# Start-up order, constants, and a last block in two column halves in a fused attention and mixture-of-experts kernel

## The chip, the cores and the metric

The kernel runs on one core of one Trainium2 chip. The metric is device microseconds of one execution; three runs of the kernel before are given, with their median. The profile is of one further execution, with a time of its own.

The engines are named as the profile names them: PE multiplies matrices (PEld is its weight load), DVE, ACT and POOL work on rows, SP issues plain transfers. Indirect transfers (gathers and scatters of rows) are issued by POOL.

## The reference

```python
scores = (q_c @ k_c.T) / sqrt(64)                 # chunks of 64 positions, per head
attn = exp(scores - scores.max(-1)); attn /= attn.sum(-1)
x = (attn @ v_c)                                  # 4608 tokens of 512
out = x.copy()
do_compute = (x @ w_skip) > 0
xc = x[do_compute]
e_idx = argmax(xc @ w_gate); gate_w = softmax(xc @ w_gate)[e_idx]      # 8 experts
for e in range(8):
    h = relu(xc[e_idx == e] @ w1[e])              # 512 -> 1024
    out[those rows] = xc[...] + gate_w * (h @ w2[e])                   # 1024 -> 512
```

## The kernel before

Attention runs over 36 tiles of 128 tokens, with heads side by side. An outer loop over i, from -1 to 40, writes one step of each stage per turn, for different tiles: scores of tile i+1 (`pe_scores`, L226, in float32, 32 small matmuls), their row maximum (`ve_max`, DVE), its subtraction by two matmuls into the same bank (`pe_sub`, L242), the exponential (`ac_exp`, ACT), the transpose of tile i-1 (`pe_ptrans`) and its eviction (`ac_pt`, ACT), the product with v (`pe_pv`), the division (`ve_norm`, DVE), the transpose of the result (`pe_xtrans`), its split into two float16 parts (`ac_xt`, ACT and POOL) and the routing logits of tile i-4 (`pe_logits`, L311). The product with v and the logits share a tile `pv` of which there is one; `pe_logits` of one tile opens it for the product of the next, so it waits until `ve_norm` has read the product before. Each engine takes its instructions in the order in which this loop writes them.

The first loads stand ahead of the loop (L163 to L173); those of later tiles are written inside it, up to three tiles ahead, each bound to the last PE instruction written so far (`paced`). Ten matmuls on zeros (`pe_warm`, L192) run on PE before the first scores. A table of constants `csb` is loaded in turn 1 (L721) and converted by `more_constants` (L209) in turn 3; the logits need its `wgs`.

From the logits groups of tiles are routed to the experts; each expert's tokens are gathered in blocks of at most 128 rows (`fetch`), transposed (`blk_xt`), multiplied with w1 (`l1_steps`) and w2 (`l2_steps`), added to the rows (`blk_out`) and scattered. Weights are split into two float16 parts, so each product is three matmuls. Blocks 0 to 3 of the first expert are computed between attention steps by a generator (`filler`); a block is open once so many half turns have passed since its gather was written: `cur[0] >= fetched[m] + F_LAG[min(m, EARLY_B)]`, with `F_LAG = (7, 6, 6, 5)` and `EARLY_B = 3`. Block 3 has 80 rows; its banks are named `eb`, those of the blocks before `fb`.

The other experts follow the attention loop, expert by expert. The last one has a single block of 112 rows. After it come a loop over blocks that overflow (`tc.For_i`, L938), whose body has no row in this trace, and behind the loop the output of the last block:

```python
    while len(prev) > 1:
        out_prev()
    ...
    with tc.For_i(0, lend, 1) as si:
        ...
    out_prev(1 << 30)
```

`prev` holds the generators of `blk_out` that are not finished; before, only that of the last block is left when the loop comes.

Of the kernel before, what the change touches and what calls it, by code (L numbers as in the profile page):

```python
# [18 lines left out]
P = 128  # L19
# [4 lines left out]
DM = H * D  # L24
# [35 lines left out]
NPRE = 18  # L60
F_LAG = (7, 6, 6, 5)
F_RATE = 1.05
# [45 lines left out]
def moe_attention_kernel(ctx: ExitStack, tc: tile.TileContext, q: bass.AP, k: bass.AP, v: bass.AP, cst: bass.AP, wall: bass.AP, out: bass.AP):  # L108
# [43 lines left out]

    def load_k(t, eng=None):
        if t < NT:
            paced((eng or nc.sync).dma_start(T[t]["qk"][:, 1], k[t]))

# [6 lines left out]
    load_q(0)  # L163
    load_k(0, nc.scalar)
    load_q(1)
    load_k(1)
    load_v(0)
    load_q(2)
    load_k(2)
    load_v(1)  # L170
    load_q(3)
    load_k(3)
# [18 lines left out]

    pe_warm(10)  # L192

# [11 lines left out]
    wgs = cpool.tile([P, KC, 2, NX], F16, name="wgs")  # L205
    reci = cpool.tile([P, NB], I32, name="reci")
    recg = cpool.tile([P, NB], F32, name="recg")

    def more_constants():  # L209
        nc.vector.tensor_copy(upper, C("upper"))  # L210
        nc.vector.tensor_copy(iota, C("iota"))
        nc.vector.tensor_scalar(wgs[:, :, 0], wg, SR, None, op0=ALU.mult)
        nc.vector.scalar_tensor_tensor(wgs[:, :, 1], wg, SR, wgs[:, :, 0], op0=ALU.mult, op1=ALU.subtract)
        nc.gpsimd.tensor_copy(vals[:, :, 0], C("tok"))
        nc.gpsimd.tensor_copy(vals[:, :, 2], C("part").to_broadcast([P, NT]))
        nc.gpsimd.memset(ecum[:, 0, :], 0.0)
        nc.gpsimd.memset(rec, 0.0)
# [220 lines left out]
    def finish_records(lo, hi):  # L438
        nc.vector.scalar_tensor_tensor(reci[:, lo:hi], rec[:, 0, lo:hi], EMPTY, rec[:, 2, lo:hi], op0=ALU.add, op1=ALU.add)
        nc.vector.tensor_tensor(recg[:, lo:hi], rec[:, 1, lo:hi], rec[:, 3, lo:hi], op=ALU.add)  # L440
        nc.vector.tensor_scalar(recg[:, lo:hi], recg[:, lo:hi], 1.0 / (SGATE * SX * SW * SW), None, op0=ALU.mult)
        ready.append(hi)

# [93 lines left out]

    def l2_steps(y, ht, w, o, n, every=2):
        cg = l2_tiles(n)
        fw = FC // cg  # L540
        for f in range(fw):
            for m, (a, b) in enumerate(((0, 0), (0, 1), (1, 0))):
                for c in range(cg):
                    fc = c * fw + f
                    pe_last[0] = nc.tensor.matmul(y[c * P // cg:c * P // cg + n], ht[:, a, fc, o:o + n], w[:, b, fc, P * KC:], start=(f == 0 and m == 0), stop=(f == fw - 1 and m == 2), skip_group_check=True)  # L545
            if (f + 1) % every == 0:
                yield

    def blk_out(ys, parts, idx, gate, xg, n, rows=NTOK):
        yo = spool.tile([P, DM], F32, name="yo", bufs=3)  # L550
        for (o, m), y in zip(parts, ys):
            cg = l2_tiles(m)
            r = slice(o, o + m)
            for c in range(cg):
                nc.vector.scalar_tensor_tensor(yo[r], y[c * P // cg:c * P // cg + m], gate[r], yo[r] if c else xg[r], op0=ALU.mult, op1=ALU.add)  # L555
                yield
        rows_dma(out=out[:rows, :], out_offset=bass.IndirectOffsetOnAxis(ap=idx[:n], axis=0), in_=yo[:n], in_offset=None, bounds_check=rows - 1, oob_is_err=False)

# [135 lines left out]
    for i in range(-1, NT + 5):  # L694
# [22 lines left out]
        if i == 0 or i > 1:  # L717
            load_k(i + LOOK + (i == 0))
        on(pe_scores, i + 1)
        if i == 1:  # L720
# [4 lines left out]
        run_route("d", 600 if urgent() else 350 if not late_group() else 0)  # L725
        on(ve_max, i + 1)
        flush()
        on(pe_logits, i - 4, i - 1 if i - 1 < NT else None)
# [11 lines left out]
        fill(F_RATE if i < NT else 2)  # L740
        if i == 3:
            more_constants()
        move(extra[1:2])
        for u in CONV.get(i, ""):
# [142 lines left out]
    for u, (p, bs, offs, n) in list(enumerate(units))[1:]:  # L887
# [20 lines left out]
        for b_, o in zip(bs, offs):  # L908
            ys = []
            for po, m in parts[b_]:  # L910
                y = ps_y.tile([P, DM], F32, name="y")
# [90 lines left out]
```

## Time and profile before

| | |
|---|---|
| median of 3 runs | 338.68 us (335.71 to 340.44) |
| the profiled execution | 336.04 us, span 334.3 us |
| granted PE clock, mean | 0.994 |
| PE busy | 314.5 us, 94% of the span |
| DVE, ACT, POOL busy | 237.0, 162.6, 152.3 us |
| moved by DMA | 81.83 MB, 245 GB/s over the span |

Times of an engine are the union of its instructions. PE's instructions overlap, and their ends are modelled; a PE that is busy is not PE at its peak. What an engine waited for is inferred from semaphores.

### The profile page before, as it was taken

What the parts mean: (1) busy time and instruction counts of PE and PEld (TensorE: products, weight loads), DVE (VectorE), ACT (ScalarE), POOL (GpSimd) and SP (SyncE); (2) the same over time, 40 slices, a digit from 0 to 9 for tenths busy, and PEclk for the clock granted to TensorE, in tenths of its full rate; (3) what the DMA queues carried; (4) which work ended last, traced back from release to release, by engine and by line L of the source; (5) the groups of instructions that cost most, each with busy time, mean ns of one, the idle gap of its engine ahead of it and who ended that gap; (6) DMA issues with size and microseconds to landing.
All of it is one profiled execution on the core that took longest, in us unless ns stands there. A gap on an engine that the chain in (4) does not pass through costs nothing. (4 is left out here: it accounts for less than half of the span.)

```text
span 334.3 us, 11290 instructions
## 1 busy us (share of the span) xinstructions
PE 314.5 (94%) x4537; PEld 221.7 (66%) x4537; DVE 237.0 (71%) x566; ACT 162.6 (49%) x337; POOL 152.3 (46%) x187
## 2 busy tenths in 40 slices
PE   7989899989999998989999999999999999999991
PEld 3777777877777776656555447647647649688580
DVE  1667676685679788853489876886887999868330
ACT  2555344655565462434467454554554555456120
POOL 5166478879987971188920441231242221120111
PEclk9999999999999999999999999999999999999997
DMA  7989799999999999587823897667567676744010
GB/s 263 336 274 319 252 283 298 378 329 284 308 393 324 381 393 370 221 261 267 255 63 125 263 305 231 208 201 232 188 225 253 199 225 224 246 167 154 34 30 28
DMA packets 41320, 81.83 MB, mean 245 GB/s; under 512 B 5022, under 2 KB 5022, under 8 KB 41264
## 3 DMA queue, kind: packets, MB, share of 16 engines
q1 hardware_dynamic: 38016, 71.48, 63.7%
q0 software_dynamic: 3104, 9.33, 8.5%
q8 instruction: 37, 0.61, 0.7%
q10 hardware_dynamic: 144, 0.26, 0.2%
q14 instruction: 19, 0.16, 0.1%
HBM read 67.02 MB, written 14.17 MB: 243 GB/s over the span
## 5 line engine op out<-in xcount | busy, mean ns | idle before, releaser
L545 PE MATMUL y<-wset,ht 128*128 128x512 f16 (+7 forms) x480 | 86.2, 380 | 0.0
L486 POOL DMA_INDIRECT out<-yo,reci x22 | 24.3, 1104 | 129.9 <-DVE yo L555 115.7
L520 PEld LDWEIGHTS <-wset 128*128 128x128 f16 x768 | 64.1, 98 | 15.5 <-issue 2.6
L545 PEld LDWEIGHTS <-ht 128*128 128x128 f16 (+7 forms) x552 | 44.8, 101 | 42.3 <-issue 2.0
L796 DVE SCALAR_TENSOR_TENSOR wset<-wst,wset 128x512 f16<-128x512 f32 x96 | 61.5, 683 | 0.9 <-ACT wset L795 0.4
L520 PE MATMUL hp<-xt,wset 128*128 128x288 f16 (+4 forms) x576 | 60.5, 267 | 0.0
L795 ACT ACTIVATE wset<-wst 128x512 f16<-128x512 f32 x96 | 53.9, 620 | 3.3 <-DVE wset L796 2.2
L524 ACT ACTIVATE ht<-hp 128x288 f16<-128x288 f32 (+5 forms) x56 | 21.7, 389 | 44.5 <-PE hp L520 43.3
L239 DVE TENSOR_REDUCE mx<-sp 128x8 bf16<-128x512 f32 x36 | 24.7, 686 | 23.0 <-PE sp L234 22.9
L249 ACT ACTIVATE px<-sp 128x512 f32<-128x512 f32 x36 | 21.4, 594 | 33.6 <-PE sp L245 28.2
L512 DVE SCALAR_TENSOR_TENSOR ht<-hp,ht 128x288 f16<-128x288 f32 (+5 forms) x56 | 23.5, 428 | 17.3 <-ACT ht L524 15.4
L309 POOL TENSOR_TENSOR xh<-xs,xh 128x256 f16<-128x256 f32 (+1 forms) x45 | 34.3, 779 | 2.2
L261 ACT ACTIVATE pts<-pt 128x512 f32<-128x512 f32 x36 | 21.4, 596 | 28.1 <-PE pt L256 28.1
L273 PE MATMUL pv<-vb,pts 64*64 64x65 f32 x1152 | 27.3, 224 | 2.5 <-issue 2.2
L306 POOL CAST xh<-xs 128x512 f16<-128x512 f32 x27 | 17.0, 629 | 24.2 <-ACT xs L305 24.0
L234 PEld LDWEIGHTS sp<-qkb 64*64 64x64 f32 x1152 | 20.6, 135 | 10.9 <-ACT px L249 5.2
L234 PE MATMUL sp<-qkb 64*64 64x64 f32 x1152 | 25.7, 225 | 1.1 <-issue 0.7
L486 POOL DMA_INDIRECT xg<-out,reci x22 | 23.9, 1089 | 5.8 <-issue 4.4
L273 PEld LDWEIGHTS pv<-vb,pts 64*64 64x64 f32 x1152 | 21.5, 133 | 4.4 <-issue 3.5
L500 ACT ACTIVATE xt<-xq 128x512 f16<-128x512 f32 (+6 forms) x18 | 9.1, 512 | 29.4 <-PE xq L499 28.9
L256 PE MATMUL pt<-ident,px 128*128 128x128 f32 x144 | 22.6, 279 | 0.1
L555 DVE SCALAR_TENSOR_TENSOR yo<-y,recg,xg 128x512 f32<-128x512 f32 (+7 forms) x20 | 14.8, 742 | 7.6 <-PEq L938 5.0
(133 smaller groups left out, 461.3 us busy)
## 6 DMA issues: line engine op xcount, KB each, us to landing
wst<-in_wall SPq DMA_DIRECT2D x96, 256.0 KB
vb<-in_v SPq DMA_DIRECT2D x36, 260.0 KB
qkb<-in_q SPq DMA_DIRECT2D x36, 256.0 KB
qkb<-in_k SPq DMA_DIRECT2D x35, 256.0 KB
out<-hold SPq DMA_DIRECT2D x20, 256.0 KB
wset<-in_wall SPq DMA_DIRECT2D x16, 256.0 KB
out<-xb SPq DMA_DIRECT2D x16, 256.0 KB
wset<-in_wall SPq DMA_DIRECT2D x8, 512.0 KB
```

Of the source, the lines that this page charges most:

```text
L234: pe_last[0] = nc.tensor.matmul(sp[halves[a], c, j * CH:(j + 1) * CH], qk[halves[c], 0, w], qk[halves[c], 1, w], start=(j == 0), stop=Fals ...
L239: nc.vector.tensor_reduce(mx, T[t]["sp"][:, :, :KC * CH].rearrange("p c (j s) -> p c j s", s=CH), axis=AX.X, op=ALU.max, negate=True)
L256: pe_last[0] = nc.tensor.transpose(pt[:, j, :], px[:, j * P:(j + 1) * P], ident)
L273: pe_last[0] = nc.tensor.matmul(pv[halves[c], jj, m * VW:(m + 1) * VW], pt[halves[jj], c * 2 + jp, halves[a]], vv[halves[jj], c * KC + m, ...
L309: nc.gpsimd.tensor_tensor(xh[:, 1, w], xs[:, w], xh[:, 0, w], op=ALU.subtract)
L486: ins = nc.gpsimd.indirect_dma_start(**kw)
L512: nc.vector.scalar_tensor_tensor(ht[:, 1, fc, :n], hp, 0.0, ht[:, 0, fc, :n], op0=ALU.max, op1=ALU.subtract)
L520: pe_last[0] = nc.tensor.matmul(hp, w()[:, a, fc, j * P:(j + 1) * P], xt[:, b, j, :n], start=(m == 0), stop=(m == 11))
L524: nc.scalar.activation(ht[:, 0, fc, :n], hp, AF.Relu)
L545: pe_last[0] = nc.tensor.matmul(y[c * P // cg:c * P // cg + n], ht[:, a, fc, o:o + n], w[:, b, fc, P * KC:], start=(f == 0 and m == 0), st ...
L795: nc.scalar.activation(w[:, 0, fc, r], st[part], AF.Copy, scale=SW)
L796: nc.vector.scalar_tensor_tensor(w[:, 1, fc, r], st[part], SW, w[:, 0, fc, r], op0=ALU.mult, op1=ALU.subtract)
```

## The change

Six edits. (1) The first loads all go through SP, in the order q0, k0, q1, k1, q2, k2, v0, q3, v1, k3, v2. (2) Nine matmuls on zeros in place of ten. (3) The scores of tile 1 are written in turn -1, behind those of tile 0, ahead of the first subtraction. (4) `wgs` is made in turn 2 by ACT and POOL (not in turn 3 by DVE); the rest of the constants in turn 5 by ACT and POOL. (5) `F_LAG` of block 3 is 6 half turns, not 5. (6) The last block's second layer runs as two halves of 256 columns, each with its own bank, output and scatter; the row numbers of the scatter are doubled (`recl`) and the output is seen as rows of 256.

```diff
-F_LAG = (7, 6, 6, 5)
+F_LAG = (7, 6, 6, 6)
...
     load_q(0)
-    load_k(0, nc.scalar)
+    load_k(0)
     load_q(1)
     load_k(1)
-    load_v(0)
     load_q(2)
     load_k(2)
+    load_v(0)
+    load_q(3)
     load_v(1)
-    load_q(3)
     load_k(3)
     load_v(2)
...
-    pe_warm(10)
+    pe_warm(9)
...
+    recl = cpool.tile([P, 2], I32, name="recl")
...
     def more_constants():
-        nc.vector.tensor_copy(upper, C("upper"))
-        nc.vector.tensor_copy(iota, C("iota"))
-        nc.vector.tensor_scalar(wgs[:, :, 0], wg, SR, None, op0=ALU.mult)
-        nc.vector.scalar_tensor_tensor(wgs[:, :, 1], wg, SR, wgs[:, :, 0], op0=ALU.mult, op1=ALU.subtract)
+        nc.scalar.activation(wgs[:, :, 0], wg, AF.Copy, scale=SR)
+        nc.gpsimd.tensor_scalar(wg, wg, SR, 1.0, op0=ALU.mult, op1=ALU.mult)
+        nc.gpsimd.tensor_tensor(wgs[:, :, 1], wg, wgs[:, :, 0], op=ALU.subtract)
+
+    def row_constants():
+        nc.scalar.activation(upper, C("upper"), AF.Copy)
+        nc.scalar.activation(iota, C("iota"), AF.Copy)
         nc.gpsimd.tensor_copy(vals[:, :, 0], C("tok"))
...
+        if hi == NB:
+            for z in range(2):
+                nc.vector.tensor_scalar(recl[:, z:z + 1], reci[:, NB - 1:], 2.0, float(z), op0=ALU.mult, op1=ALU.add)
...
-    def l2_steps(y, ht, w, o, n, every=2):
+    def l2_steps(y, ht, w, o, n, every=2, cols=(0, DM)):
...
-                    pe_last[0] = nc.tensor.matmul(y[c * P // cg:c * P // cg + n], ht[:, a, fc, o:o + n], w[:, b, fc, P * KC:], start=(f == 0 and m == 0), stop=(f == fw - 1 and m == 2), skip_group_check=True)
+                    pe_last[0] = nc.tensor.matmul(y[c * P // cg:c * P // cg + n, :cols[1] - cols[0]], ht[:, a, fc, o:o + n], w[:, b, fc, P * KC + cols[0]:P * KC + cols[1]], start=(f == 0 and m == 0), stop=(f == fw - 1 and m == 2), skip_group_check=True)
...
-            on(pe_scores, i + 1)
+        if i:
+            on(pe_scores, i + 1)
...
         on(ve_max, i + 1)
+        if i < 0:
+            pe_scores(1)
         flush()
...
-        if i == 3:
+        if i == 2:
             more_constants()
+        if i == 5:
+            row_constants()
...
+            if b_ == NB - 1:
+                for z, cols in enumerate(((0, DM // 2), (DM // 2, DM))):
+                    y = ps_y.tile([P, DM], F32, name="y")
+                    for _ in l2_steps(y, hc, w, o, rows_of[b_], cols=cols):
+                        take(steps, 1)
+                        out_prev()
+                    prev.append(blk_out([y], parts[b_], recl[:, z:z + 1], recg[:, b_:b_ + 1], xgs[b_], rows_of[b_], CUT_ROWS, cols))
+                continue
```

The row numbers of the places below are the kernel's own, so those of after are some lines higher (L234 is L238 there, L245 is L249, L256 is L260, L486 is L493, L499 is L506, L545 is L552, L938 is L962). PE at the start, before: the end of the matmuls on zeros, the scores of tile 0 (`sp_150`), their subtraction, then the scores of tile 1 (`sp_175`) and the first transpose.

```order
L190 MATMUL xt_108<-zeros_97 128x512
L234 MATMUL sp_150<-qkb_83 64x64 x16
L245 LDWEIGHTS identb_104
L245 MATMUL sp_150<-mx_167,identb_104 128x256
...
L234 MATMUL sp_175<-qkb_83 64x64 x16
L256 MATMUL pt_194<-ident_103,px_171 128x128 x4
L245 LDWEIGHTS identb_104
L245 MATMUL sp_175<-mx_192,identb_104 128x256
```

The same stretch of PE after; the scores of tile 1 are `sp_169` here.

```order
L190 MATMUL xt_108<-zeros_97 128x512
L238 MATMUL sp_150<-qkb_83 64x64 x16
L238 MATMUL sp_169<-qkb_83 64x64 x16
L249 LDWEIGHTS identb_104
L249 MATMUL sp_150<-mx_167,identb_104 128x256
...
L260 MATMUL pt_194<-ident_103,px_188 128x128 x4
L249 LDWEIGHTS identb_104
L249 MATMUL sp_169<-mx_192,identb_104 128x256
```

The scores of tile 1 have moved ahead of the subtraction of tile 0; between that subtraction and the first transpose nothing is left.

PE where block 3 is transposed, before: behind the logits of one tile come the four transposes of the 80 gathered rows (`eb_3397<-ident_103,xg_3266`), then second-layer matmuls of an earlier block (`fb_3370`) and the transpose of an attention tile (`xt_3412`).

```order
L320 LDWEIGHTS xh_3299
L320 MATMUL pv_3380<-wgs_125,xh_3299 128x9
L499 MATMUL eb_3397<-ident_103,xg_3266 128x80 x4
L545 LDWEIGHTS ht0_147
L545 MATMUL fb_3370<-wset_144,ht0_147 128x512
...
L294 MATMUL xt_3412<-ident_103,xb_82 128x128 x4
```

The same stretch after; the transposes of the gathered rows are `eb_3419<-ident_103,xg_3269`.

```order
L324 LDWEIGHTS xh_3302
L324 MATMUL pv_3383<-wgs_124,xh_3302 128x9
L552 LDWEIGHTS ht0_147
L552 MATMUL fb_3373<-wset_144,ht0_147 128x512
...
L298 MATMUL xt_3407<-ident_103,xb_82 128x128 x4
L506 MATMUL eb_3419<-ident_103,xg_3269 128x80 x4
```

The transposes of the gathered rows now stand behind six second-layer matmuls (the rows left out are five more like the one shown) and the transpose of the attention tile. Of the eight first-layer groups of block 3, which before stand four between other work and four alone at the end, two now stand between and six alone.

POOL at the end, before: the scatter of the block before the last (`yo_5599`), the load of the overflow count, the branches of the overflow loop, its body, and behind it the last scatter (`yo_6151`).

```order
L486 DMA out_0<-yo_5599,reci_126 3456x512
L937 TENSOR_LOAD nend_4955
L938 COMPARE_AND_BRANCH
...
L938 UNCONDITIONAL_BRANCH
L486 DMA out_0<-yo_6151,reci_126 3456x512
L996 UNCONDITIONAL_BRANCH
```

The same after: the two scatters of the last block are `yo_5744` and `yo_6184`, with the row numbers `recl_126`.

```order
L493 DMA out_0<-yo_5602,reci_125 3456x512
L493 DMA out_0<-yo_5744,recl_126 6912x256
L961 TENSOR_LOAD nend_4958
L962 COMPARE_AND_BRANCH
...
L962 UNCONDITIONAL_BRANCH
L493 DMA out_0<-yo_6184,recl_126 6912x256
L1020 UNCONDITIONAL_BRANCH
```

The scatter of the first half stands ahead of the loop, that of the second half behind it.

## Rows read from the trace of the kernel before

**Rows 1.** The page: busy time of each engine, share of the span, instructions.

```profile
PE 314.5 (94%) x4537; PEld 221.7 (66%) x4537; DVE 237.0 (71%) x566; ACT 162.6 (49%) x337; POOL 152.3 (46%) x187
```

**Rows 2.** Stretches: length, busy time and instructions per engine, PE clock, DMA share, GB/s.

```profile
0.00:20.00 20.00, 16.32 (x377) 11.21 (x378) 9.35 (x24) 7.51 (x13) 9.02 (x25) 1.00 0.87 301
...
80.00:100.00 20.00, 20.00 (x441) 15.54 (x434) 13.12 (x39) 12.04 (x26) 18.28 (x22) 1.00 0.99 341
```

**Rows 3.** Timeline of the first turns: start, duration, engine, instruction, [idle before].

```profile
1.24 4.45 PE L190 MATMUL xt<-zeros 128*128 128x512 f16 x10 [1.24 <-DVE zeros L176]
...
5.61 0.66 PEld L234 LDWEIGHTS sp<-qkb 64*64 64x64 f32 x32 [0.84 <-issue]
...
8.30 0.42 PEld L256 LDWEIGHTS pt<-ident,px 128*128 128x128 f32 x4 [0.20 <-ACT px L249]
...
8.31 0.69 DVE L239 TENSOR_REDUCE mx<-sp 128x8 bf16<-128x512 f32 x1 [1.12 <-PE sp L234]
...
9.06 0.38 PE L245 MATMUL sp<-mx,identb 128*128 128x256 bf16 x2
```

**Rows 4.** The line of the scores up to 6.45 us: durations min/median/max, first and last start.

```profile
L234 PE MATMUL sp<-qkb x32: 218/218/366, 5.6 to 6.2; 64*64 64x64 f32 x32
L234 PEldq EVENT_SEMAPHORE  x1: 51/51/51, 4.4 to 4.4; - x1
```

**Rows 5.** All DMA of the first 12 us.

```profile
DMA packets 1891, 3.48 MB, mean 290 GB/s; under 512 B 206, under 2 KB 206, under 8 KB 1890
```

**Rows 6.** Timeline from 13 to 19 us.

```profile
13.34 0.60 ACT L261 ACTIVATE pts<-pt 128x512 f32<-128x512 f32 x1 [1.10 <-PE pt L256]
...
15.73 0.22 DVE L210 CAST upper<-csb 128x128 f16<-128x128 f32 x1
...
15.93 1.31 POOL L309 TENSOR_TENSOR xh<-xs,xh 128x256 f16<-128x256 f32 x2
...
16.69 0.60 DVE L213 SCALAR_TENSOR_TENSOR wgs<-csb,wgs 128x36 f16<-128x36 f32 x1
...
17.65 0.69 DVE L283 TENSOR_TENSOR hold<-pv,rr 128x512 f32<-128x512 f32 x1
...
18.45 0.10 PEld L319 LDWEIGHTS <-xh 128*128 128x128 f16 x1 [1.20 <-POOL xh L306]
```

**Rows 7.** Timeline around block 3's transposes and its last first-layer group.

```profile
148.69 0.50 PE L499 MATMUL eb<-ident,xg 80*128 80x80 f32 x4 [0.98 <-DMA xg<-out,reci]
...
158.44 0.59 PE L520 MATMUL eb<-xt,wset 128*128 128x80 f16 x12 [0.22 <-DVE ht L512]
```

**Rows 8.** Timeline of the end.

```profile
319.44 1.01 POOL L486 DMA_INDIRECT out<-yo,reci  x1 [5.67 <-DVE ht L512]
...
321.97 5.35 PE L545 MATMUL y<-wset,ht 128*112 128x512 f16 x24
...
327.72 0.75 DVE L555 SCALAR_TENSOR_TENSOR yo<-y,recg,xg 112x512 f32<-112x512 f32 x1 [4.98 <-PEq L938]
328.75 0.95 POOL L486 DMA_INDIRECT out<-yo,reci  x1 [8.29 <-DVE yo L555]
```

**Rows 9.** Groups by line and shape near the end: xcount | busy us, mean ns | idle.

```profile
L520 PE MATMUL hp<-xt,wset 128*128 128x232 f16 x66 | 6.7, 263 | 0.0
...
L512 DVE SCALAR_TENSOR_TENSOR ht<-hp,ht 128x112 f16<-128x112 f32 x8 | 2.1, 272 | 4.2 <-ACT ht L524 4.2
```

**Rows 10.** Stretch of the last scatter's packets (columns as in rows 2).

```profile
330.20:331.30 1.10, 0.00 (x0) 0.00 (x0) 0.00 (x0) 0.00 (x0) 0.00 (x0) 0.50 0.63 196
```

**Rows 11.** The overflow loop's line on POOL, 321.2 to 322.8 us.

```profile
L938 POOLq EVENT_SEMAPHORE  x3: 43/43/1253, 321.2 to 321.4; - x3
```

**Rows 12.** The same line on DVE, 323.9 to 327.6 us.

```profile
L938 DVEq EVENT_SEMAPHORE  x12: 49/50/2444, 323.9 to 325.0; - x12
```

**Rows 13.** The program's last line on SP, 328 to 333 us.

```profile
L996 SPq EVENT_SEMAPHORE  x1: 17/17/17, 331.6 to 331.6; - x1
```

**Rows 14.** The same line on POOL, 328 to 333.4 us.

```profile
L996 POOLq DRAIN  x1: 4954/4954/4954, 328.5 to 328.5; - x1
```

More of the change, by code (lines that the diff above doesn't have):

```diff
@@ L151, in load_q, with load_k @@
             paced(nc.sync.dma_start(T[t]["qk"][:, 0], q[t]))
-    def load_k(t, eng=None):
+    def load_k(t):
         if t < NT:
-            paced((eng or nc.sync).dma_start(T[t]["qk"][:, 1], k[t]))
+            paced(nc.sync.dma_start(T[t]["qk"][:, 1], k[t]))
     def load_v(t):
@@ L544, in l2_steps, with blk_out @@
                     fc = c * fw + f
-                    pe_last[0] = nc.tensor.matmul(y[c * P // cg:c * P // cg + n], ht[:, a, fc, o:o + n], w[:, b, fc, P * KC:], start=(f == 0 and m == 0), stop=(f == fw - 1 and m == 2), skip_group_check=True)
+                    pe_last[0] = nc.tensor.matmul(y[c * P // cg:c * P // cg + n, :cols[1] - cols[0]], ht[:, a, fc, o:o + n], w[:, b, fc, P * KC + cols[0]:P * KC + cols[1]], start=(f == 0 and m == 0), stop=(f == fw - 1 and m == 2), skip_group_check=True)
             if (f + 1) % every == 0:
                 yield
-    def blk_out(ys, parts, idx, gate, xg, n, rows=NTOK):
+    def blk_out(ys, parts, idx, gate, xg, n, rows=NTOK, cols=(0, DM)):
+        d = slice(*cols)
         yo = spool.tile([P, DM], F32, name="yo", bufs=3)
@@ L554, in blk_out @@
             for c in range(cg):
-                nc.vector.scalar_tensor_tensor(yo[r], y[c * P // cg:c * P // cg + m], gate[r], yo[r] if c else xg[r], op0=ALU.mult, op1=ALU.add)
+                nc.vector.scalar_tensor_tensor(yo[r, d], y[c * P // cg:c * P // cg + m, :cols[1] - cols[0]], gate[r], yo[r, d] if c else xg[r, d], op0=ALU.mult, op1=ALU.add)
                 yield
-        rows_dma(out=out[:rows, :], out_offset=bass.IndirectOffsetOnAxis(ap=idx[:n], axis=0), in_=yo[:n], in_offset=None, bounds_check=rows - 1, oob_is_err=False)
+        to = out[:rows, :]
+        if cols[1] - cols[0] < DM:
+            to, rows = to.rearrange("r (z d) -> (r z) d", z=2), 2 * rows
+        rows_dma(out=to, out_offset=bass.IndirectOffsetOnAxis(ap=idx[:n], axis=0), in_=yo[:n, d], in_offset=None, bounds_check=rows - 1, oob_is_err=False)
     def on(f, t, *a):
```

## The prediction

> **What bounds the kernel now.** I read the page first: PE is busy 94% of the span [rows 1]. Then the stretches, where a row such as 80 to 100 us shows it at 20.00 of 20 us [rows 2]. So PE's order of work sets the length, and whatever delays PE or the work behind its last matmul counts fully, while DVE (71%), ACT and POOL matter where PE waits for them. PE is not full at three places that the change touches: the start, block 3's transposes, and the end. I read each on the timeline, with the waits of the line behind it. No more than a few microseconds are at stake, out of 336.
>
> The sums are made against the profiled execution, 336.04 us (span 334.3, so 1.7 outside). It is one of four executions shown, 335.71, 336.04, 338.68 and 340.44; their middle is (336.04 + 338.68) / 2 = 337.4. The same kernel thus spreads over 4.7 us. I put the sum on that middle; about 2%, 6.8 us, is what a measurement of this kernel can tell from no change.
>
> **The start: nine matmuls on zeros, loads in order.** PE's ten matmuls on zeros run from 1.24 for 4.45 us, and the weights of the first scores wait 0.84 us and come at 5.61, just as they end [rows 3]. One of the scores' two load waits was over at 4.4 [rows 4], before the last of those matmuls ended. So the scores wait for the matmuls on zeros, not for the loads, and k0 can land some 0.4 us later than now (SP issues it second) without cost; if it came at 5.6 the gain of this edit would be nil, and that is its lower bound.
>
> One matmul on zeros less is 4.45 / 10 = 0.44 us. But the matmuls of the scores take up to 366 ns at first and 218 in the median [rows 4]: PE reaches its full speed only during them, around 5.8. If that comes at the same time, what is brought forward runs at half speed and half is kept: 0.2 us. Bounds 0 and 0.44; I take 0.2, since the slow rows lie exactly there. [...]
>
> **Second scores ahead of the first subtraction.** The subtraction of tile 1 stands at 9.06, after the maximum of tile 1 (8.31 for 0.69 us, which had waited 1.12 us for the scores). PE had loaded the transposes' weights by 8.30 + 0.42 = 8.72 [rows 3]. With the scores of tile 1 written earlier, that maximum falls into the 0.8 us in which PE waits for the first one, and the subtraction can follow the transposes: 9.06 - 8.72 = 0.34 us. Bounds 0 (the maxima queue on DVE) and 0.7 (the scores' own time drops out). I take 0.34; with 0.2 it makes 0.5 us ahead. v0 and v1 move back one or two places in a queue that feeds the later pv; I cost that at nothing, because the first pv comes two stages after the scores. If that cover were gone, it is one transfer, some 0.7 us.
>
> **The constants.** csb is the 14th transfer to be issued. The first 12 us move 3.48 MB [rows 5], 13.3 transfers of 0.26 MB, so I estimate that it lands between 12.6 and 14; that it is there by 15.73 is all that the rows show, since L210 starts then without a wait [rows 6]. After, ACT's copy into wgs stands ahead of the eviction of tile 2's transpose, which starts at 13.34 now [rows 6] and 0.5 us earlier in the new timing. If csb lands at 13.0 or earlier nothing is lost; at 14 ACT stands still until then and the 0.5 us are gone again, with the exponential of tile 3 and the first xs queued behind it. POOL's two operations on 36 columns are free: POOL waits there for ACT.
>
> What leaves DVE: four operations, from 15.73 to 16.69 + 0.60 = 17.29, 1.6 us. Behind them stands the division of tile 2, which ends at 17.65 + 0.69 = 18.34. The logits of tile 0 come at 18.45 after 1.20 us idle [rows 6]. The view names POOL's L306, but what ends just before is the division, and the logits need the one pv tile which it reads. Without the four operations the division ends 1.6 us earlier, at 16.8; next in line is POOL's xh, ready at 15.93 + 1.31 = 17.24. So the logits start near 17.2, which is 1.2 us sooner, of which 0.5 was counted. I add 0.8 (bounds 0 and 1.2). Together the start gives 1.3 us, between 0.2 and 2.0. Later loads are bound to PE's own progress and move with it, and from then on PE is the bound, so what is gained stays. The other constants add two copies to ACT and four small operations to POOL in turn 5: 0 to 0.3 us, I take 0.1. The two operations for recl stand on DVE, which is idle soon after: 0.
>
> **Block 3 half a turn later.** PE waits 0.98 us for the gather ahead of the four transposes [rows 7]. Six second-layer matmuls at 5.35 / 24 = 0.22 us [rows 8] now stand ahead, 1.3 us, so the wait goes. But six first-layer groups instead of four stand alone at the end, with two banks, and each there pays up to 0.22 us [rows 7] for its bank; DVE's output of the block before (0.75 us) falls between them too. I charge two groups and part of that, 0.5 us. Net gain 0.5; bounds 1.0 gained and 0.4 lost.
>
> **The two halves at the end.** The intention: the first half's output and scatter run beside the second half's matmuls, and only half the output and half the bytes lie behind PE. 232 columns take 6.7 / 66 = 0.10 us [rows 9], so 256 take 0.11, and 48 matmuls cost what 24 of 512 cost. Half an output lies between 0.27 us (112 columns) [rows 9] and 0.75 [rows 8]: 0.44, which saves 0.31. POOL's 0.95 us of descriptors is per row and stays. The last scatter's packets lie within 1.1 us [rows 10], so half the bytes save 0 to 0.5; I take 0.25.
>
> But the second half's output stands behind the overflow loop, and each engine passes that loop by waiting for every semaphore, those of scatters included. POOL's wait of 1253 ns there [rows 11] ends at 322.7, when the scatter issued at 319.44 [rows 8] lands; DVE works through its list of waits from 323.9 to 325.0 at some 0.1 us each and then waits 2.44 us for PE [rows 12]. So now PE's end releases the output, at 327.72. After, the first half's scatter is a new member of that list. Its time: 321.97 + 24 x 0.11 = 324.6, output to 325.2, POOL 0.3 later and 0.95 us long, 326.5. From the end of the issue to landing it is 331.6 - 329.70 = 1.9 us [rows 8, 13], less up to 0.5 for half the bytes: 327.9 to 328.4. It stands near the head of the list, so DVE has some nine waits left, 0.9 us, and 0.25 to its output: 329.0 to 329.6, against 327.72. That is 1.3 to 1.8 later; minus 0.31 and 0.25 the end comes 1.0 us later. Bounds: 0.4 lost at the least by these numbers (-0.3 if the wait stands last), 1.6 at the most if POOL's drain, which runs from 328.5 to 333.5 [rows 14], hangs on the issue and not on the bytes.
>
> **Sum.** -1.3 + 0.1 - 0.5 + 1.0 = -0.7 us: 335.3 on the profiled execution, 336.7 on the middle.
>
> **The rivals.** (a) The start's gain is lost because csb holds ACT. For: ACT takes instructions in order and csb is the 14th transfer. Against: even then DVE's 1.6 us are gone. Start -0.3 in place of -1.3: sum +0.3, 337.7. (b) On the other side: the loop's waits cost more than everything gained. Place: the first half's scatter in the list ahead of the last output. Price: the scatter of 319.44 took 3.2 us from issue to landing, against 2.4 to 2.9 assumed, and the drain hangs on the issue: +2.3, with the rest at -1.7 a sum of +0.6, or 338.0; it decides once the end loses over 1.7. (c) The halves work as written, the loop's wait being met before PE ends: end -0.6, sum -2.3, 335.1. Against: the row of POOL [rows 11] shows a wait for a scatter that is 3.2 us old, and the new one is issued an us before PE's end. (d) The bank waits of block 3 eat its gain: +0.4 there, sum +0.2, 337.6.
>
> **How the numbers follow.** Forecast 0.5, (a) 0.17, (b) 0.13, (c) 0.12, (d) 0.08. All ends of the terms together give -3.3 to +2.3, both unlikely; the cases lie between 335.1 and 338.0. A median of a few runs can fall up to 1.7 off the middle, as the four executions do on their lower side (337.4 - 335.71). So 334.0 to 339.6 is the range. No case comes near 6.8 us, so within 2% gets 0.92; the rest is for what no row shows.
>
> **What would show it.** Right: the first scores near 5.2 and the logits of tile 0 near 17.2; no wait of 0.98 us at the eb transposes; a first scatter near 325.5 and a last output more than 1 us after PE's last matmul. Wrong: an ACT wait for csb, gaps in front of the late eb groups, or a last output within 0.5 us of PE's end. The number is wrong if the shifted start sets other loads against each other over the attention turns, which the rows of before can't show.

## The result and the profile after

The kernel after took 340.81 us, median of 22 executions (337.89 to 344.46), against 337.38 of the kernel before beside it (22 executions, 334.45 to 340.44). The ratio is 1.0104, 95% interval 1.008 to 1.0128: some 3.4 us slower, above the predicted range (334.0 to 339.6). The profiled execution, 344.46 us with a span of 342.6, is the longest of the 22, and ratios leave executions out whose clock was disturbed; so its rows are read for order and waits, and a second profile of the same kernel (label after_here, 337.23 us) stands beside it where lengths matter.

The page of the kernel after, busy time of each engine (before: [rows 1]):

```profile
PE 319.3 (93%) x4560; PEld 227.6 (66%) x4560; DVE 235.8 (69%) x565; ACT 163.1 (48%) x340; POOL 153.5 (45%) x190
```

PE is busy 4.8 us more in this execution, and little more work was given to it. In after_here it is busy no longer than before:

```profile
PE 314.1 (94%) x4560; PEld 223.9 (67%) x4560; DVE 237.3 (71%) x565; ACT 162.9 (49%) x340; POOL 153.1 (46%) x190
```

The stretches of the profiled execution say why it is the longest (columns as in [rows 2]; the third from the right is the granted clock):

```profile
0.00:20.00 20.00, 16.32 (x336) 11.46 (x336) 6.96 (x17) 7.30 (x14) 7.11 (x20) 0.83 0.81 260
20.00:40.00 20.00, 18.59 (x488) 15.93 (x489) 12.47 (x41) 9.61 (x21) 11.95 (x22) 0.91 0.88 278
...
60.00:80.00 20.00, 16.19 (x354) 12.73 (x353) 14.32 (x45) 9.22 (x19) 17.71 (x24) 0.91 0.92 312
80.00:100.00 20.00, 20.00 (x456) 15.73 (x454) 11.30 (x29) 11.34 (x23) 16.75 (x20) 1.00 0.86 270
```

For parts of the first 80 us PE's granted clock was 0.50 (9 to 14, 29 to 31, 53 to 55 and 77 to 79 us; before, it was 1.00 in both stretches shown), and from 60 to 80 PE was busy only 16.19 of 20. From 80 on it is full again. So what was lost in front of 80 us is lost for good. That is this one execution, though: in after_here the granted clock is 1.00 in each of these stretches. From 60 to 80 us, before and then in after_here:

```profile
60.00:80.00 20.00, 18.45 (x446) 15.16 (x437) 14.86 (x44) 11.03 (x22) 16.65 (x22) 1.00 0.97 336
```

```profile
60.00:80.00 20.00, 18.07 (x426) 14.77 (x429) 15.49 (x44) 11.32 (x23) 17.70 (x24) 1.00 0.94 319
```

The start, on the timeline of the kernel after (columns as in [rows 3]):

```profile
1.24 3.77 PE L190 MATMUL xt<-zeros 128*128 128x512 f16 x9 [1.24 <-DVE zeros L176]
...
4.94 0.69 PE L238 MATMUL sp<-qkb 64*64 64x64 f32 x32
...
7.40 0.69 PE L238 MATMUL sp<-qkb 64*64 64x64 f32 x32 [1.76 <-DMA qkb<-in_k]
...
8.02 0.61 PE L249 MATMUL sp<-mx,identb 128*128 128x256 bf16 x2
...
9.32 0.90 PE L260 MATMUL pt<-ident,px 128*128 128x128 f32 x3 [0.69 <-ACT px L253]
```

The first scores come at 4.94 (5.18 in after_here, as predicted). Then PE stands 1.76 us for k of tile 1 (0.86 in after_here), with the subtraction of tile 0 behind the waiting scores, although its maximum was there at 6.39 (5.70 for 0.69 on DVE). Behind that idle time the granted clock is 0.50 (from 8.2 us on), and the subtraction takes 0.61 us, 0.38 in [rows 3] (0.39 in after_here, where the granted clock of the first 20 us is 1.00). The constants and the first logits, later in the same timeline (before: [rows 6], logits at 18.45):

```profile
14.84 0.24 ACT L211 ACTIVATE wgs<-csb 128x36 f16<-128x36 f32 x1
...
19.77 0.18 PE L323 MATMUL pv<-wgs,xh 128*128 128x18 f16 x1
```

In after_here ACT waits 1.60 us for csb ahead of that copy, and the logits come at 17.52 all the same, 0.9 earlier than before.

Block 3, where [rows 7] had a wait of 0.98 us ahead of the four transposes; none is left:

```profile
154.97 1.46 PE L552 MATMUL fb<-wset,ht 128*128 128x512 f16 x6
156.26 0.60 PE L298 MATMUL xt<-ident,xb 128*128 128x128 f32 x4
156.69 0.44 PE L506 MATMUL eb<-ident,xg 80*128 80x80 f32 x4
```

POOL around its first gather of expert rows:

```profile
55.60 1.31 POOL L313 TENSOR_TENSOR xh<-xs,xh 128x256 f16<-128x256 f32 x2
59.54 1.25 POOL L493 DMA_INDIRECT xg<-out,reci  x1 [2.63 <-DVE rs L283]
60.81 0.66 POOL L310 CAST xh<-xs 128x512 f16<-128x512 f32 x1
```

In the trace of before the same gather follows the same xh after 0.17 us. The releaser named here has nothing to do with it: the program's wait is for `reci`, which DVE had written by 52.79, and for rows of `out` that had landed.

The end, timeline (before: [rows 8]):

```profile
328.77 5.41 PE L552 MATMUL y<-wset,ht 128*112 128x256 f16 x48
...
331.60 0.48 DVE L563 SCALAR_TENSOR_TENSOR yo<-y,recg,xg 112x256 f32<-112x256 f32 x1 [2.05 <-PE y L552]
...
332.36 0.95 POOL L493 DMA_INDIRECT out<-yo,recl  x1 [5.09 <-DVE yo L563]
...
336.31 0.48 DVE L563 SCALAR_TENSOR_TENSOR yo<-y,recg,xg 112x256 f32<-112x256 f32 x1 [4.23 <-issue]
...
337.07 0.94 POOL L493 DMA_INDIRECT out<-yo,recl  x1 [3.76 <-DVE yo L563]
```

And the waits of the overflow loop's line and of the program's last line (before: [rows 12, 14]):

```profile
L962 DVEq EVENT_SEMAPHORE  x13: 21/50/1024, 332.4 to 336.0; - x13
L1020 POOLq DRAIN  x3: 46/114/4937, 336.8 to 342.4; - x3
```

PE ends at 328.77 + 5.41 = 334.18, and the last output starts 2.13 us later; before it was 327.72 - 327.32 = 0.40. DVE's list is as long as before, 12 waits (the thirteenth in the row stands ahead of the list; the window of [rows 12] leaves it out). What is new is that its second wait, 1.02 us, is held up; ten more follow it. In after_here that wait ends at 327.85, and the first half's scatter lands at 327.81.

### The profile page after: what moved, and what is told of

Same layout as the page of the kernel before. It is cut to its first block, busy times and chain, and to the rows that moved or that the text cites. A ratio compares the mean times of both kernels' runs of the same rounds, so it can differ in the third digit from the quotient of the medians.

```text
span 342.6 us, 11346 instructions
## 1 busy us (share of the span) xinstructions
PE 319.3 (93%) x4560; PEld 227.6 (66%) x4560; DVE 235.8 (69%) x565; ACT 163.1 (48%) x340; POOL 153.5 (45%) x190
## 5 line engine op out<-in xcount | busy, mean ns | idle before, releaser
L552 PE MATMUL y<-wset,ht 128*128 128x512 f16 (+7 forms) x504 | 86.3, 369 | 0.0
L493 POOL DMA_INDIRECT out<-yo,reci x21 | 23.4, 1113 | 121.2 <-DVE yo L563 107.0
L552 PEld LDWEIGHTS <-ht 128*128 128x128 f16 (+7 forms) x576 | 46.9, 102 | 40.7 <-issue 2.0
L238 PEld LDWEIGHTS sp<-qkb 64*64 64x64 f32 x1152 | 21.8, 143 | 13.4 <-issue 6.9
L238 PE MATMUL sp<-qkb 64*64 64x64 f32 x1152 | 27.0, 234 | 3.3 <-DMA qkb<-in_k 1.8
L277 PE MATMUL pv<-vb,pts 64*64 64x65 f32 x1152 | 26.7, 229 | 2.2 <-issue 2.0
L493 POOL DMA_INDIRECT xg<-out,reci x22 | 24.0, 1090 | 8.3 <-issue 4.9
L260 PE MATMUL pt<-ident,px 128*128 128x128 f32 x144 | 24.0, 292 | 0.7 <-ACT px L253 0.7
L277 PEld LDWEIGHTS pv<-vb,pts 64*64 64x64 f32 x1152 | 21.5, 138 | 3.3 <-issue 2.5
```

Of the source, the lines that this page charges most:

```text
L238: pe_last[0] = nc.tensor.matmul(sp[halves[a], c, j * CH:(j + 1) * CH], qk[halves[c], 0, w], qk[halves[c], 1, w], start=(j == 0), stop=Fals ...
L260: pe_last[0] = nc.tensor.transpose(pt[:, j, :], px[:, j * P:(j + 1) * P], ident)
L277: pe_last[0] = nc.tensor.matmul(pv[halves[c], jj, m * VW:(m + 1) * VW], pt[halves[jj], c * 2 + jp, halves[a]], vv[halves[jj], c * KC + m, ...
L493: ins = nc.gpsimd.indirect_dma_start(**kw)
L552: pe_last[0] = nc.tensor.matmul(y[c * P // cg:c * P // cg + n, :cols[1] - cols[0]], ht[:, a, fc, o:o + n], w[:, b, fc, P * KC + cols[0]:P ...
```

## The experiments

All ratios are against the kernel before, run beside the kernel in question on one chip. "Stall" is the time between the end of POOL's xh and its first gather; "tail" runs from the start of the last first-layer matmul to the end of the span. Both are of the one profiled execution. Medians of different rows come from different chips. Before: stall 0.17, tail 12.39 us.

| kernel | ratio (95%) | median us | stall | tail |
|---|---|---|---|---|
| start_back | 1.0035 (1.0001 to 1.0068) | 338.60 | 2.99 | 13.93 |
| scores_back | 1.0082 (1.005 to 1.0115) | 339.41 | 2.65 | 14.04 |
| loads_back | 1.007 (1.0032 to 1.0109) | 339.53 | 2.43 | 13.94 |
| halves_only | 1.0043 (1.0003 to 1.0082) | 338.40 | 0.18 | 14.05 |
| const_flag | 0.9984 (0.9939 to 1.003) | 337.46 | 2.95 | 12.45 |
| const_dve | 0.9988 (0.9951 to 1.0026) | 336.16 | 0.17 | 12.46 |
| flag_only | 0.9968 (0.9926 to 1.001) | 336.28 | 0.17 | 12.38 |
| bridge | 1.013 (1.0075 to 1.0185) | 341.68 | 3.31 | 13.93 |
| start_only | 0.999 (0.9947 to 1.0033) | 337.84 | 0.17 | 12.40 |
| scores_only | 1.0017 (0.9977 to 1.0057) | 338.13 | 0.18 | 12.59 |
| loads_only | 0.9995 (0.9964 to 1.0027) | 337.05 | 0.17 | 12.45 |
| both_behind | 1.0028 (0.9993 to 1.0064) | 337.95 | 0.17 | 13.42 |
| after_dve | 1.0037 (0.9987 to 1.0086) | 339.10 | 0.17 | 13.95 |
| whole_end | 1.0002 (0.9949 to 1.0055) | 337.82 | 2.73 | 12.59 |
| whole_dve | 0.999 (0.9933 to 1.0047) | 337.38 | 0.17 | 12.38 |
| pool_pad | 1.0024 (0.9969 to 1.0079) | 338.65 | 3.13 | 12.46 |
| after_here | 1.0145 (1.0102 to 1.0188) | 341.66 | 2.35 | 13.94 |
| after_dve_here | 1.0054 (1.0018 to 1.0089) | 338.69 | 0.17 | 14.02 |

My first theory: the start costs some 2.5 us by itself (the wait for k1 and the clock behind it), the end 1.5, and block 3 gives 0.6. The rival: the moved constants or the one queue carry the loss.

**start_back.** Edits 1 to 3 undone in the kernel after, that is the loads, `pe_warm(10)` and `on(pe_scores, i + 1)` in turn 0 as before.

> The kernel after, with the three edits of the start undone (loads, ten matmuls on zeros, scores of tile 1 in turn 0); the constants, block 3 and the two halves stay. Theory: the start is where the time went (about +2.5 us of the +3.4), the end costs 1.5, block 3 gives 0.6: 337.4 + 1.5 - 0.6 = 338.3 us, less up to 0.8 if the constants bring the logits of tile 0 forward (before: 18.45 us), so 337.5 to 338.3; granted clock 0.99, no gap of over 1.5 us on PE in the first 20 us. Rival (the loss comes from the moved constants or the end): 340 or more.

The ratio falls by 0.7%, as the theory wants. The constants bring the logits of tile 0 to 17.99 us, 0.46 earlier, but ACT stood in between, as rival (a) had it:

```profile
14.73 0.24 ACT L211 ACTIVATE wgs<-csb 128x36 f16<-128x36 f32 x1 [2.38 <-DMA csb<-in_cst]
```

**scores_back and loads_back.** One edit undone each:

```diff
-        if i:
-            on(pe_scores, i + 1)
+        on(pe_scores, i + 1)
...
-        if i < 0:
-            pe_scores(1)
```

> The kernel after with one edit undone: the scores of tile 1 are written in turn 0 again, behind the subtraction of tile 0; the loads stay in order on one queue. Theory (place): PE waited 1.76 us for k1 in front of work that was ready, and fell to the lower clock; with the old place the subtraction of tile 0 starts at about 6.4 us (8.0 in the kernel after), k1 is needed only after it, and the start's loss of about 2.5 us goes: 338.3 us. Rival (queue): k1 lands late because all loads go through one queue, 7.3 us against 5.8; then PE still waits about 0.5 to 1 us for it one step later, and the time is 339.5 to 340.5.

```diff
-    load_k(0)
+    load_k(0, nc.scalar)
     load_q(1)
     load_k(1)
+    load_v(0)
     load_q(2)
     load_k(2)
-    load_v(0)
-    load_q(3)
     load_v(1)
+    load_q(3)
```

> The kernel after with one edit undone: the order of the loads of before, k0 issued by ACT; nine matmuls on zeros and the scores of tile 1 ahead of the first subtraction stay. Queue theory: k1 lands at 5.8 us as before, the second scores wait 0.2 us or less, the clock stays at 1.00 and the time is 338.3 us. Place theory: those scores have no room left, so any late part of k1 is waited for; gap in front of them 0.3 to 1.7 us, and part of the loss stays: 339 to 340.5.

Neither gets the 0.7% back, so neither "place" nor "queue" alone was the answer. At the start both were cured (the maximum of tile 3 at 11.92 and 11.49 us; 12.03 before, 15.24 after), yet both were behind the kernel before by 5.2 and 5.8 us at tile 21: in these two executions the loss had moved to 25 to 75 us. They are the longest and the second longest of their kernels, and the lag at tile 21 says little of a kernel: flag_only (ratio 0.9968) is 1.7 us behind there and pool_pad (1.0024) 9.2.

**halves_only.** Edit 6 alone in the kernel before.

> The kernel before with only the two halves of the last block. Theory: the output of the second half waits in the list ahead of the overflow loop for the landing of the first half's scatter: about 2 us between PE's last matmul and that output (0.4 before), drain of POOL as long behind the scatter as before; +1.5 us: 338.9. Rival (the halves work as written, or cost nothing): 336.8 to 337.4.

The theory of the end holds. The tail in the table is the same in every kernel with the two halves as in the change, 13.91 to 14.05 us, and 12.38 to 12.59 in every kernel with one: 1.5 us, whatever came before it.

**const_flag, const_dve, flag_only.** Edits 4 and 5 alone in the kernel before; the same with the second part of `wgs` on DVE; and `F_LAG = (7, 6, 6, 6)` alone. The second differs from the first in

```diff
-        nc.gpsimd.tensor_scalar(wg, wg, SR, 1.0, op0=ALU.mult, op1=ALU.mult)
-        nc.gpsimd.tensor_tensor(wgs[:, :, 1], wg, wgs[:, :, 0], op=ALU.subtract)
+        nc.vector.scalar_tensor_tensor(wgs[:, :, 1], wg, SR, wgs[:, :, 0], op0=ALU.mult, op1=ALU.subtract)
```

> The kernel before with the constants moved and F_LAG 6 alone (old start, whole last block). If the parts add up, start_back less halves_only: ratio 0.999, about 335.7 us against 336.0 of before. Theory of the code page: POOL has three instructions more ahead of its first gather; that gather starts some 3 us after the xh ahead of it has ended (0.17 us before), right behind a load of 8 KB of code, the logits of a tile then wait 1 to 1.5 us for POOL, and the gain of block 3 (0.6) and of the first logits is lost there. Rival (POOL's late gather was chance): the gather follows at once and the time is 334.9 to 335.3.

> const_flag with the second part of wgs made by one operation on DVE, not by two on POOL, so that POOL has as many instructions ahead of its first gather as in the kernel before. Theory of the code page: the gather starts within 0.3 us of the end of the xh ahead of it, PE has no wait for POOL there, and the time is 1 us or more below const_flag: 334.5 to 335. Rival (it isn't the place in the code): 3 us before the gather as in start_back, time as const_flag.

> The kernel before with F_LAG 6 for block 3 alone. Theory: the wait of 0.98 us ahead of the four transposes goes and 0.4 comes back at the late groups: 0.6 us less, 335.4 us against 336.0. Rival (the bank waits eat it): 336.0 to 336.4.

The stall went as expected, from 2.95 us to this, the timeline of const_dve:

```profile
50.39 1.31 POOL L311 TENSOR_TENSOR xh<-xs,xh 128x256 f16<-128x256 f32 x2
51.87 1.24 POOL L488 DMA_INDIRECT xg<-out,reci  x1 [0.17 <-issue]
```

The times did not tell the two apart. flag_only is the lowest of all, but its interval reaches 1.001; no kernel here is shown to beat the kernel before.

**bridge.** The kernel after with PE kept at work in the wait for k1:

```diff
         if i < 0:
+            pe_warm(7)
             pe_scores(1)
```

> The kernel after with seven more matmuls on zeros between the scores of tile 0 and those of tile 1, in the wait of 1.76 us for k1. Theory of the clock: PE stood still there and fell to the lower clock for the next turns; with the matmuls the granted clock of the first 20 us is 0.95 or more (0.83 in the kernel after), the maximum of tile 3 comes at 12 to 13.5 us (15.24), and the time falls by 1.5 to 2.5 us against the kernel after: ratio to before 1.003 to 1.006 (1.0104). Rival (the clock falls for another reason, or what is gained early is lost again by tile 20): ratio 1.009 to 1.011.

Its first stretch:

```profile
0.00:20.00 20.00, 16.73 (x370) 11.17 (x374) 7.52 (x17) 7.64 (x14) 7.38 (x21) 1.00 0.84 274
```

The granted clock held at 1.00 and the maximum of tile 3 came at 12.91. That fits an idle time in front of the second scores that brings the clock down, but the idle time alone does not decide it: with 1.76, 1.11 and 1.14 us (after, after_dve, whole_dve) the clock fell in the execution (0.83 over the first 20 us of after; 0.987 and 0.979 in the mean of the other two), with 1.45 and 0.86 us (after_dve_here, after_here) it held (0.995 in the mean; 1.00 over the first 20 us). The time did not fall. The theory that the start carries the loss through this clock is down.

**start_only, scores_only, loads_only.** Edits 1 to 3, edit 3 and edit 1 alone in the kernel before.

> The kernel before with the three edits of the start alone: loads in order on one queue, nine matmuls on zeros, scores of tile 1 ahead of the first subtraction. The kernel after (ratio 1.0104) less start_back (1.0035) leaves 0.7% for them. Theory (they cost by themselves, through the wait for k1 and the lower clock behind it): ratio 1.005 to 1.009, 338.3 to 339.6 us with before at 336.6; the maximum of tile 3 comes 1 us or more later than the 12.03 of before. Rival (they cost only together with the moved constants, which then wait for csb on ACT): ratio 0.998 to 1.002.

> The kernel before with the scores of tile 1 ahead of the first subtraction, the loads in their old order with k0 issued by ACT. Theory of the place: k1 lands at 5.8 to 6.2 us, the second scores wait 0.2 to 0.8 us for it and the subtraction of tile 0 stands behind them, but the clock holds; ratio 1.001 to 1.004. Rival (as predicted for the kernel after: 0.34 us gained and kept): ratio 0.999.

> The kernel before with the first loads in the new order on one queue alone; scores of tile 1 and ten matmuls on zeros as before. Theory: k1 lands about 7 us, when the subtraction of tile 0 has been done at 7.2, so the scores wait little; ratio 1.000 to 1.003. Rival (the late v0 and v1, or the one queue, shift the loads against each other over the attention turns): ratio 1.004 to 1.007 with the loss between 20 and 75 us.

None loses anything that can be measured. The ratio of start_only lies where its rival wanted it, but the reason that the rival gives, start and moved constants together, is not borne out: whole_end below has both and shows no loss either. Nor is a gain shown: the predicted 1.3 us would be a ratio of 0.996, which the interval of start_only does not exclude. Its timeline shows where that gain is missing in one execution:

```profile
5.19 1.13 PE L234 MATMUL sp<-qkb 64*64 64x64 f32 x32
...
6.78 0.69 PE L234 MATMUL sp<-qkb 64*64 64x64 f32 x32 [0.46 <-DMA qkb<-in_k]
...
7.40 0.39 PE L245 MATMUL sp<-mx,identb 128*128 128x256 bf16 x2
...
8.98 0.38 PE L245 MATMUL sp<-mx,identb 128*128 128x256 bf16 x2
```

The first scores start 0.43 us earlier and take 1.13 us, in place of 0.80 (in the trace of before, from 5.62), so the maximum of tile 0 gains 0.11 (6.39; 6.50 before). The subtraction of tile 0, ready at 7.08 (its maximum is on DVE from 6.39 for 0.69), stands behind the scores of tile 1 until 7.40; in the trace of before it started at 7.24. The subtraction of tile 1 comes at 8.98, 0.08 earlier than in [rows 3]. At tile 3 the two kernels are level, 12.02 and 12.03.

**both_behind.** halves_only with both outputs and scatters behind the overflow loop:

```diff
-                        out_prev()
+                        if z == 0 or len(prev) > 1:
+                            out_prev()
...
-    while len(prev) > 1:
+    while len(prev) > 2:
```

> halves_only with the output and the scatter of the first half written behind the overflow loop as well, beside those of the second. Theory of the list: without a scatter of the last block outstanding, the list is passed as in the kernel before, and the first output starts 0.3 to 0.5 us after PE's last matmul (2.1 in the kernel after); two outputs of 0.48 us and two scatters of 0.95 in a row then end the program 0.6 to 0.8 us later than in the kernel before, behind the same last matmul: ratio 1.002, 0.8 us less than halves_only. Rival (what costs is the second scatter itself): ratio as halves_only, 1.0043.

Its end:

```profile
321.31 5.41 PE L549 MATMUL y<-wset,ht 128*112 128x256 f16 x48
...
327.12 0.88 DVE L560 SCALAR_TENSOR_TENSOR yo<-y,recg,xg 112x256 f32<-112x256 f32 x2 [5.04 <-PEq L955]
...
327.88 0.95 POOL L490 DMA_INDIRECT out<-yo,recl  x1 [8.10 <-DVE yo L560]
...
329.14 0.94 POOL L490 DMA_INDIRECT out<-yo,recl  x1 [0.30 <-issue]
```

PE ends at 326.72 and the outputs start at 327.12, 0.40 later as in the kernel before: without a scatter of this block in flight the list costs nothing. The tail is 13.42, 1.03 over before (expected 0.6 to 0.8): the second scatter and the 0.30 us ahead of it cost 1.24, and the first scatter is issued 0.27 earlier, the output being half as long. The ratio lies between those of before and of halves_only and can't be told from either.

**after_dve, whole_end, whole_dve, pool_pad.** The first three are the kernel after with the edit of const_dve, without the halves, and with both. The last puts the stall alone into the kernel before:

```diff
         nc.gpsimd.memset(ecum[:, 0, :], 0.0)
+        for _ in range(3):
+            nc.gpsimd.memset(ecum[:, 0, :], 0.0)
```

> The kernel after with the second part of wgs made by one operation on DVE, so that POOL has as many instructions ahead of its first gather as in the kernel before. Theory of the code page: the gather follows the xh ahead of it within 0.3 us (2.7 to 3.0 in the kernel after), PE's waits for POOL's xh near 60 us (1.5 us in sum) go, and the ratio falls from 1.0104 to 1.004 to 1.007. Rival (the stall is paid elsewhere anyway, the loss sits in the start): 1.009 or more.

> The kernel after without the halves: last block whole, one output and one scatter behind the overflow loop. The end costs 1.5 us (0.46%) by the stretch behind the last first-layer matmul: ratio 1.0058, between 1.004 and 1.0075. Rival (the parts add up as measured alone, 0.999 and 0.998): 0.996 to 0.999.

> whole_end with the second part of wgs on DVE: start, constants and block 3 of the kernel after, without the end and without the stall of POOL. Theory of the code page: ratio 0.998 to 1.001. Rival (loss in the start): 1.004 to 1.007, as whole_end.

> The kernel before with three more memsets of the same 9 columns on POOL among the constants of turn 3 (they set again what is set there, 0.1 us each). Theory of the code page: the first gather starts some 3 us after the xh ahead of it (0.17 in the kernel before), behind a load of 8 KB of code, and PE waits 1.3 to 1.9 us for POOL's xh near 58 us; ratio 1.003 to 1.006. Rival (it was the kind or the place of the moved operations): the gather follows at once, ratio 1.000.

Three memsets, 40 us ahead of the place (17.71 to 18.16), bring the stall. POOL and then PE in pool_pad:

```profile
56.70 1.30 POOL L311 TENSOR_TENSOR xh<-xs,xh 128x256 f16<-128x256 f32 x2
61.13 1.24 POOL L488 DMA_INDIRECT xg<-out,reci  x1 [3.13 <-DVE xb L285]
...
63.06 0.18 PE L321 MATMUL pv<-wgs,xh 128*128 128x18 f16 x1 [1.36 <-POOL xh L308]
63.81 0.18 PE L322 MATMUL pv<-wgs,xh 128*128 128x9 f16 x1 [0.56 <-POOL xh L311]
...
64.59 1.14 PE L275 MATMUL pv<-vb,pts 64*64 64x65 f32 x32
```

And a row of its DMA queues from 58.1 to 61.1 us, inside the stall (queue and kind: packets, MB, share):

```profile
q14 instruction: 1, 0.01, 0.6%
```

That is one load of 8 KB of instructions. PE waits 1.36 and 0.56 us for xh, and the product behind it takes 1.14 us, where one in the kernel after took 0.70 (PE L277, 58.38). By their ratios pool_pad (expected 1.003 to 1.006), whole_end and whole_dve can't be told from no change; the 1.0058 expected of whole_end lies just outside its interval. So start, constants, block 3 and the stall together show no loss as long as the last block is whole.

**after_here, after_dve_here.** The kernel after and after_dve once more, beside each other.

> The kernel after, unchanged, beside after_dve on one chip. If the loss is one of the kernel and not of a chip: ratio 1.008 to 1.012; if its parts just add up: 1.002 to 1.006. In its trace POOL's first gather starts 2.7 to 3.1 us after the xh ahead of it.

> after_dve once more: the second part of wgs on DVE, no stall of POOL. Theory (the stall carries what the end does not): 0.4 to 0.6% below after_here, ratio 1.004 to 1.006. Rival (the stall is paid in a wait that would come anyway): within 0.2% of after_here.

With the stall 1.0145 (from 6 executions), without it 1.0054: 0.9% or 3 us between kernels that differ only in where one part of `wgs` is made, and the intervals do not meet, if barely. What is left, 0.54%, is about what the end costs (1.5 of 336 us is 0.45%).

The parts do not add up. Taken out of the kernel after one at a time, the start (start_back), POOL's two operations (after_dve) and the halves (whole_end) each bring the ratio down by 0.7 to 1.0%. Put alone into the kernel before, the start, the constants with block 3, the stall (start_only, const_flag, pool_pad) and the halves measure -0.2 to +0.4%. Only the 0.45% of the end is accounted for, by the tails and by halves_only; why the rest, some 2 us, needs the edits together, no run shows.

## Why the prediction was wrong

The change measured +3.4 us, against a sum of -0.7. With the start at nothing and the end at 1.5 the prediction's own sum would be +1.1; the other 2.3 us appear only with the edits together. That the stall of POOL carries them is argued: the kernel after and its twin on DVE say so twice, two other pairs do not.

**The start, predicted -1.3 us, gave nothing that can be measured.** The step that failed is "that maximum falls into the 0.8 us in which PE waits for the first one". It looked at the gap and not at k1: I had checked how late k0 may land, and never when k1 does. In the new order k1 is the fourth transfer on one queue; in the eight traces of kernels with both edits the second scores waited 0.46 to 1.76 us (bridge fills that gap with other work), and the subtraction of tile 0 behind them. For the 0.2 us for one matmul less, start_only shows 0.11, since the first scores took longer (1.13 us), but one pair of executions can't settle it: PE went over to its faster rate anywhere between 4.25 and 7.25 us (the half speed in that term is 0.44 us for a matmul on zeros [rows 3], 0.22 for a second-layer matmul of the same 128x512 [rows 8]), and the maximum of tile 0 starts at 5.52 to 6.39 us in the ten traces with nine matmuls (mean 6.09) and at 5.84 to 6.82 in the ten with ten (mean 6.47), so the means are 0.38 apart. Of the 0.8 us for the logits, start_back shows 0.46, and after_here 0.9 of all that the start was to bring (18.45 to 17.52); rival (a), ACT held by csb, was right about the wait (2.38 us). And "what is gained stays" rested on a stretch, 80 to 100 us, in which PE is full. Between 20 and 80 us it is not, in the kernel before either (18.29, 18.54 and 18.45 of 20 us): scores_back, loads_back and bridge each had the start mended and were 5 us behind at tile 21 all the same, in long executions.

**The constants, predicted +0.1, stall POOL; what that costs is not settled.** The step that failed is "POOL's two operations on 36 columns are free". I costed POOL's operations by their length. What counts is that there are two more of them (three instructions with their wait) ahead of POOL's first gather. Nine traces (of eight kernels) have them or the three memsets, with 69 instructions ahead of the gather, which starts 2.35 to 3.31 us late, with the 8 KB load inside the stall in each; eleven (of ten kernels, the one before among them) have 66, the gather starts after 0.17 or 0.18 us, and the load comes behind its start. From the maximum of tile 17 to that of tile 22 the nine take 24.9 us in the mean and the eleven 21.8; but six of the nine executions are the longest or second longest of their kernels, two of the eleven, so the 3.1 us are not the stall's price. So the stall is shown, and that it depends on how many instructions stand ahead. Its price is not settled: 0.7 and 0.9% between the kernel after and its twin on DVE, but no more than 0.2% in const_flag against const_dve and in whole_end against whole_dve, where the intervals are 0.4 to 0.6% wide to each side. In the profile of after_here it cost PE about 1 us, and yet the last first-layer matmul starts at 321.46, 0.46 earlier than in the trace of before: what that execution loses (337.23 against 336.04 us) is the end.

**Block 3, predicted -0.5 (bounds -1.0 and +0.4): right in kind.** The wait is gone, and from the maximum of tile 35 to the last product of block 3 the 13 traces with 6 half turns take 21.2 to 21.8 us, those with 5 take 22.0 to 22.7, but for halves_only with 21.15, which found the rows there. The means are some 0.8 us apart. In the time it is not shown: flag_only's interval reaches 1.001.

**The end, predicted +1.0 (bounds -0.3 and +1.6), cost 1.5.** The mechanism was right: the last output started 2.13 us after PE's end, so 1.7 later than before, within the 1.3 to 1.8 stated. It is not that the list has a new member, as the prediction put it; a wait that stood in it was held up (in after_here the first scatter starts at 325.10, predicted near 325.5). POOL's 0.95 us stayed with half the columns: 0.95 and 0.94 for the two scatters of the kernel after. The mis-sized term is the 0.25 us for half the bytes. POOL's drain ends 3.76 us behind the issue of the last scatter in the kernel after (337.07 + 0.94 = 338.01; 336.84 + 4.94 = 341.78) and 3.76 before (329.70; 333.45 by [rows 14]); it hangs on the issue, not on the bytes, which the prediction kept as its bound. both_behind shows the other half of it, that a second scatter costs a whole one.

**The range** held only what happens at the three places that the change touches. What the moved constants did to POOL 40 us later was in none of its cases; the sentence on the attention turns at its end allowed for loads set against each other, and instructions were among those loads. Two sums of the text do not come out as stated, and nothing hangs on them: the worst ends of the terms add up to +2.1, not +2.3, and the cases less and plus 1.7 give 333.4 to 339.7. Rival (b) had the right place for the end, but it set the price against gains of the start that never came.

## What to carry to other kernels

Before work is moved ahead of a waiting step, read when its own input lands, not only how long the engine stands there. The loop here, with an output behind it, waited for the scatter still in flight, so splitting the output ahead of it lost 1.5 us: look for such a wait before splitting. A few instructions more on an engine can move the place where it loads its next instructions onto a step that others wait for (here 69 in place of 66 on POOL, and the first gather 2.35 to 3.31 us late); when a harmless edit shows a stall far from where it was made, look for a load of instructions there. And edits that measure nothing alone can cost together, so a bundle is to be taken apart from both sides.

## What the hardware showed that I had not expected

PE's idle times that no semaphore explains stand at fixed instructions. I counted PE's instructions in 20 traces (two each of the kernel after and of after_dve). Of 143 idle times of over 0.5 us between 10 and 140 us, 65 end at an instruction that waits on nothing, and the number of every one of these is 193 more than a multiple of 256 (449, 961, 1217, 1473, 2241, ...). All others end at a wait on a semaphore. The longest of the 65 was 2.65 us (whole_end, at 27.84), and which of the places is hit differs from execution to execution: in the two profiles of the kernel after 961 and 2241, and 961, 1729 and 4801. To each of them belongs a load of 16 KB on queue q8, kind instruction, and in the ten cases that I followed PE goes on 2.2 to 2.7 us after it starts (36.40 and 38.67 in the trace of before; 49.07 and 51.52 after); over all 65 it is 2.2 to 3.7 us. That the idle time is the wait for this load was argued from these places, not tried.

In the first 80 us of the kernel after the DMA engines were busy 0.81 to 0.92 of the time, and PE stood still at two of these places in that execution, 1.30 and 2.04 us. The load inside POOL's stall is of 8 KB (queue q14).

Behind idle times of this kind PE was slow more than once, so the time lost is more than the gap: in halves_only, 1.43 us idle at 58.29, then transposes of 1.11 us (0.66 in the kernel after, 59.01); in the kernel after, 2.04 us idle up to 51.52, then a granted clock of 0.50 from 52.8 to 55.8 us. That single executions of one kernel lie 5 us and more apart fits this; no run took it apart.
